# Window-attention backward: from 16x8 token tiles with on-array transposes to stacked 8x8 pairs with DMA transposes

## Chip, core and metric

One NeuronCore of one Trainium2 chip runs the whole program. The metric is the device time of one execution in microseconds (us), the median over runs. Below, PE is the matrix engine (with PEld its weight loads), DVE the vector engine, ACT the scalar engine, POOL and SP the two engines that here mostly issue DMAs.

## What is computed

The image has 256x256 tokens with 384 channels. It is cut into 8x8 windows; within each window there is softmax attention over its 64 tokens, forward and backward:

```python
xw  = windows(x)                                   # [1024 windows, 64 tokens, 384]
q, k, v = split(xw @ wqkv)                         # wqkv [384, 1152]
p   = softmax(q @ k.T * 384**-0.5)                 # 64x64 per window
out = unwindow((p @ v) @ wo)                       # wo [384, 384]
_, vjp = jax.vjp(f, x, wqkv, wo)
return out, *vjp(grad_out)                         # out, dx, dwqkv, dwo
```

All arrays are bfloat16; four results are written.

## The kernel before

Both kernels first fold the weights: A = scale*Wq*Wk^T and its transpose give scores from x alone, and B = Wv*Wo and its transpose give the output and the gradient, so no q, k or v is ever formed. The weight gradients are accumulated as x^T U and x^T W in float32 (`G_acc`, `F_acc`) and turned into dwqkv and dwo after the loop.

Before, a tile is 128 tokens: 8 rows by 16 columns of the image, that is two windows side by side whose tokens are interleaved (8 of one, 8 of the other). The 128x128 score matrix therefore has both windows' scores in a checkerboard, and a fourth matmul (`maskU`, `maskV`, L221) adds a large negative number where the windows cross. The loops run over 32 bands of 8 rows (`band_body`), 4 quads of 4 tiles in each band (128 quads of 512 tokens in all), and in each quad the stages `stage_f1`, `stage_f2`, `stage_b1`, `stage_b2`, `stage_b3` over its 4 tiles. For each quad:

- L173 and L175 load x and grad_out (SP and POOL issue), L180 and L182 transpose them on PE, L183 copies them out of PSUM.
- L190 and L196 project the quad by A and B (rows of 512 columns); L210 transposes the second result back.
- L216 scores, L224 exponential, L244 transposes P, L248 forms the output, L259 to L273 the score gradient, L277 and L282 the operands U and W of the weight gradient, L300 and L305 three transposed products, and L316 the nine matmuls of dx.
- After every 16 tiles, L331 runs 6 chains of 16 matmuls (`ps_dw`) for the weight gradients.

Tile pools give the buffers, and a scheduler of the framework sets the order of instructions on each engine, interleaving neighbouring quads. The quads are written out in full: the program has no loop at run time.

Of the kernel before, what the change touches and what calls it, by code (L numbers as in the profile page):

```python
# [8 lines left out]
ACT = mybir.ActivationFunctionType  # L9
ALU = mybir.AluOpType  # L10
AX = mybir.AxisListType
# [5 lines left out]
def kernel(  # L17
# [10 lines left out]
    dynamic_loop: bool = True,  # L28
    TPB: int = 4,
    NBI: int = 32, HINT_ENGINES=(),  # L30
    GRPN: int = 16, MASK_MM: bool = True, YT_ACT: bool = False, WT_ACT: bool = False, SMALL_ACT: bool = False, XB_ACT: bool = False,
):
    nc = tc.nc
    B, H, W, C = x.shape
    assert B == 1
    P = 128
    CK = C // P
    assert CK * P == C
    WIN = 8
    NB = H // WIN  # L40
    TW = 16
    NTB = W // TW
    assert NTB * TW == W and NB * WIN == H
    QUAD = min(4, NTB)
    GRP = min(GRPN, NTB)
    assert NTB % GRP == 0 and GRP % QUAD == 0
    NGB = NTB // GRP
    QPG = GRP // QUAD
    scale = float(C) ** -0.5
    J = 3 * C  # L50
    JK = J // P
    NBI = min(NBI, NB)
    while NB % NBI != 0:
        NBI -= 1

    const = ctx.enter_context(tc.tile_pool(name="const", bufs=1))
    setup = ctx.enter_context(tc.tile_pool(name="setup", bufs=1))
    qpool = ctx.enter_context(tc.tile_pool(name="qpool", bufs=2))
    gpool = ctx.enter_context(tc.tile_pool(name="gpool", bufs=2))
    tp = ctx.enter_context(tc.tile_pool(name="tp", bufs=TPB))  # L60
    sp = ctx.enter_context(tc.tile_pool(name="sp", bufs=2 * TPB))
    psq = ctx.enter_context(tc.tile_pool(name="psq", bufs=2, space=bass.MemoryType.PSUM))
    psf1 = ctx.enter_context(tc.tile_pool(name="psf1", bufs=1, space=bass.MemoryType.PSUM))
    psf2 = ctx.enter_context(tc.tile_pool(name="psf2", bufs=1, space=bass.MemoryType.PSUM))
    psb1 = ctx.enter_context(tc.tile_pool(name="psb1", bufs=1, space=bass.MemoryType.PSUM))
    psb2 = ctx.enter_context(tc.tile_pool(name="psb2", bufs=1, space=bass.MemoryType.PSUM))
    psb3 = ctx.enter_context(tc.tile_pool(name="psb3", bufs=1, space=bass.MemoryType.PSUM))
    psdw = ctx.enter_context(tc.tile_pool(name="psdw", bufs=1, space=bass.MemoryType.PSUM))

    ident = const.tile([P, P], BF16)  # L70
    make_identity(nc, ident[:])

    w_sb = const.tile([P, CK, J], BF16)
    nc.sync.dma_start(out=w_sb[:], in_=wqkv.rearrange("(m p) j -> p m j", p=P))
    wo_sb = setup.tile([P, CK, C], BF16)
    nc.scalar.dma_start(out=wo_sb[:], in_=wo.rearrange("(m p) n -> p m n", p=P))

    wqkvT_sb = setup.tile([P, JK, C], BF16, tag='setup_big')
    for jm in range(JK):
        ps_t = psq.tile([P, C], BF16, tag="q")  # L80
        for m in range(CK):
            nc.tensor.transpose(ps_t[:, m * P:(m + 1) * P], w_sb[:, m, jm * P:(jm + 1) * P], ident[:])
        nc.vector.tensor_copy(out=wqkvT_sb[:, jm, :], in_=ps_t[:])
    woT_sb = const.tile([P, CK, C], BF16)
    for mco in range(CK):
        ps_t = psq.tile([P, C], BF16, tag="q")
        for mc in range(CK):
            nc.tensor.transpose(ps_t[:, mc * P:(mc + 1) * P], wo_sb[:, mc, mco * P:(mco + 1) * P], ident[:])
        nc.vector.tensor_copy(out=woT_sb[:, mco, :], in_=ps_t[:])

    Bm_sb = const.tile([P, CK, C], BF16)
    for mcin in range(CK):
        ps_c = psq.tile([P, C], F32, tag="q")
        for mc in range(CK):
            nc.tensor.matmul(ps_c[:], lhsT=wqkvT_sb[:, 2 * CK + mc, mcin * P:(mcin + 1) * P], rhs=wo_sb[:, mc, :],
                             start=(mc == 0), stop=(mc == CK - 1))
        nc.vector.tensor_copy(out=Bm_sb[:, mcin, :], in_=ps_c[:])
    A1_sb = const.tile([P, CK, C], BF16)
    for mcin in range(CK):
        ps_c = psq.tile([P, C], F32, tag="q")  # L100
        for mc in range(CK):
            nc.tensor.matmul(ps_c[:], lhsT=wqkvT_sb[:, CK + mc, mcin * P:(mcin + 1) * P], rhs=wqkvT_sb[:, mc, :],
                             start=(mc == 0), stop=(mc == CK - 1))
        nc.scalar.activation(out=A1_sb[:, mcin, :], in_=ps_c[:], func=ACT.Copy, scale=scale)
    A2_sb = const.tile([P, CK, C], BF16)
    for mcin in range(CK):
        ps_c = psq.tile([P, C], F32, tag="q")
        for mc in range(CK):
            nc.tensor.matmul(ps_c[:], lhsT=wqkvT_sb[:, mc, mcin * P:(mcin + 1) * P], rhs=wqkvT_sb[:, CK + mc, :],
                             start=(mc == 0), stop=(mc == CK - 1))  # L110
        nc.scalar.activation(out=A2_sb[:, mcin, :], in_=ps_c[:], func=ACT.Copy, scale=scale)
    A3_sb = const.tile([P, CK, C], BF16)
    for mco in range(CK):
        ps_c = psq.tile([P, C], F32, tag="q")
        for mc in range(CK):
            nc.tensor.matmul(ps_c[:], lhsT=wo_sb[:, mc, mco * P:(mco + 1) * P], rhs=wqkvT_sb[:, 2 * CK + mc, :],
                             start=(mc == 0), stop=(mc == CK - 1))
        nc.vector.tensor_copy(out=A3_sb[:, mco, :], in_=ps_c[:])

    u_f = const.tile([1, P], F32)  # L120
    nc.gpsimd.iota(u_f[:], pattern=[[0, 8], [1, 2], [0, 8]], base=0, channel_multiplier=0,
                   allow_small_or_imprecise_dtypes=True)
    u_b = const.tile([1, P], BF16)
    nc.vector.tensor_scalar(out=u_b[:], in0=u_f[:], scalar1=-2.0, scalar2=1.0, op0=ALU.mult, op1=ALU.add)
    ps_m = psq.tile([P, P], F32, tag="q")
    nc.tensor.matmul(ps_m[:], lhsT=u_b[:], rhs=u_b[:], start=True, stop=True)
    u2_f = const.tile([P, P], F32)
    nc.gpsimd.iota(u2_f[:], pattern=[[0, 8], [1, 2], [0, 8]], base=0, channel_multiplier=4,
                   allow_small_or_imprecise_dtypes=True)
    maskU = const.tile([P, P], BF16)  # L130
    maskV = const.tile([P, P], BF16)
    tmpm = const.tile([P, P], F32)
    nc.vector.tensor_scalar(out=tmpm[:], in0=u2_f[:], scalar1=-2.0, scalar2=1.0, op0=ALU.mult, op1=ALU.add)
    nc.gpsimd.affine_select(out=tmpm[:], in_=tmpm[:], pattern=[[0, P]], compare_op=ALU.is_ge, fill=0.0,
                            base=0, channel_multiplier=-1)
    nc.vector.tensor_copy(out=maskU[:], in_=tmpm[:])
    nc.vector.tensor_scalar(out=maskV[:], in0=tmpm[:], scalar1=2048.0, scalar2=None, op0=ALU.mult)
    nmask = const.tile([P, P], F32)
    nc.vector.tensor_scalar(out=nmask[:], in0=ps_m[:], scalar1=-15000.0, scalar2=15000.0, op0=ALU.mult, op1=ALU.add)

    G_acc = const.tile([P, CK, C], F32)
    F_acc = const.tile([P, CK, C], F32)
    nc.vector.memset(G_acc[:], 0.0)
    nc.gpsimd.memset(F_acc[:], 0.0)

    def dram_tile(ap, b, bt):
        if isinstance(b, int):
            rows = slice(WIN * b, WIN * b + WIN)
        else:
            rows = bass.ds(b * WIN, WIN)  # L150
        return ap[0, rows, TW * bt:TW * bt + TW, :]

    def iter_body(it):
        for sbi in range(NBI):
            b = it * NBI + sbi
            band_body(b)

    def band_body(b):
        for grp in range(NGB):
            x_toks = []  # L160
            do_toks = []
            U_sbs = []
            W_sbs = []
            for q in range(QPG):
                bt0 = grp * GRP + q * QUAD
                xdT_quad = qpool.tile([P, 2, CK, QUAD * P], BF16)
                xT_quad = xdT_quad[:, 0, :, :]
                doT_quad = xdT_quad[:, 1, :, :]
                for bi in range(QUAD):
                    bt = bt0 + bi  # L170
                    gi = bt - grp * GRP
                    x_tok = gpool.tile([P, C], BF16, tag=f"x_tok{gi}")
                    nc.sync.dma_start(out=x_tok[:], in_=dram_tile(x, b, bt))  # L173
                    do_tok = gpool.tile([P, C], BF16, tag=f"do_tok{gi}")
                    nc.gpsimd.dma_start(out=do_tok[:], in_=dram_tile(grad_out, b, bt))  # L175
                    x_toks.append(x_tok)
                    do_toks.append(do_tok)
# [243 lines left out]
```

## Time and profile before

| what | value |
|---|---|
| median of 3 runs | 3115.81 us (3114.57 to 3115.82) |
| profiled execution, first to last instruction (span) | 3115.0 us |
| PE busy, PE weight loads | 3041.1 us (98%), 1867.8 us (60%) |
| DVE, ACT, POOL busy | 2020.5 (65%), 1527.4 (49%), 614.2 us (20%) |
| matmuls, all instructions | 23935, 64454 |
| DMA | 208.43 MB, mean 67 GB/s |

The profile is of one execution; its own time is known as its span, which lies inside the three runs' range. Busy time of PE counts each matmul from its start to a modelled end, and successive matmuls overlap, so 98% does not say that the array is full: the distance between the starts of neighbouring matmuls says more. A line number such as L316 is the line of the kernel that issued the instruction.

### The profile page before, as it was taken

How to read it: one execution, taken by the hardware profiler on the slowest of the kernel's cores; microseconds unless marked ns; L12 is line 12 of the kernel's file. 1: busy time of each engine (PE TensorE's matmuls, PEld its weight loads, DVE VectorE, ACT ScalarE, POOL GpSimd, SP SyncE). 2: the span in 40 equal slices, each digit the busy share in tenths (PEclk: the TensorE clock that was granted, in tenths of full speed). 3: DMA queues.
4: the chain of work that ended last, by engine and by line, in shares of the span. 5: the costliest groups of instructions: out<-in, count | busy, mean ns of one | idle time of the engine just before them, and what ended most of it. 6: DMA issues, size and time to landing. Idle time of an engine off the chain costs nothing.

```text
span 3115.0 us, 64454 instructions
## 1 busy us (share of the span) xinstructions
PE 3041.1 (98%) x23935; PEld 1867.8 (60%) x23935; DVE 2020.5 (65%) x6758; ACT 1527.4 (49%) x3981; POOL 614.2 (20%) x1034
## 2 busy tenths in 40 slices
PE   8999999999999999999999999999999999999998
PEld 5565656666666656666566656566665656656564
DVE  6666766667666666666666666766666666667665
ACT  4445544445444454444554444544445444455443
POOL 4122111122111121111211212211112111121100
PEclk9999999999999999999999999999999999999999
DMA  4222222212222122222222221222212222222211
GB/s 129 68 63 64 71 69 69 70 52 76 68 70 69 52 76 69 70 68 60 65 71 70 71 66 54 76 68 70 70 53 74 68 70 69 62 65 71 58 33 40
DMA packets 206716, 208.43 MB, mean 67 GB/s; under 512 B 49216, under 2 KB 181056, under 8 KB 206400
## 3 DMA queue, kind: packets, MB, share of 16 engines
q0 software_dynamic: 65536, 101.25, 12.2%
q1 hardware_dynamic: 140464, 102.76, 11.2%
q8 instruction: 187, 3.06, 0.4%
q14 instruction: 129, 1.06, 0.1%
q10 hardware_dynamic: 400, 0.29, 0.0%
HBM read 101.84 MB, written 101.84 MB: 65 GB/s over the span
## 4 chain that ended last, share of the span: by engine, by line
PE 88%; DVE 4%; issue 4%; ACT 3%; DMA 0%; ACTq 0%
PE ps_dx L316 24%; PE ps_dw L331 13%; PE ps_p L190 8%; PE ps_p L196 8%; PE ps_t L300 5%; PE ps_W L282 4%; PE ps_w L305 4%; PE ps_xB L210 3%; PE ps_dP L259 3%; PE ps_U L277 3%; PE ps_S L216 3%; PE ps_out L248 2%; DVE xdT_quad L183 2%; PE ps_xdT L180 2%; PE ps_xdT L182 2%
## 5 line engine op out<-in xcount | busy, mean ns | idle before, releaser
L316 PE MATMUL ps_dx<-A_sb,uvwT_sb 128*128 128x384 bf16 x3072 | 703.6, 326 | 0.1
L175 POOL DMA_DIRECT2D do_tok<-in_grad_out_dram x512 | 300.6, 588 | 1429.1 <-PE ps_w L305 1247.3
L302 ACT CAST uvwT_sb<-ps_t 128x512 bf16<-128x512 f32 (+1 forms) x1024 | 498.9, 487 | 85.8 <-PE ps_t L300 82.4
L321 POOL DMA_DIRECT2D out_dram<-dx_sb x512 | 311.2, 608 | 1040.5 <-ACT dx_sb L320 1008.0
L284 DVE CAST W_sb<-ps_W 128x384 bf16<-128x384 f32 x512 | 284.2, 555 | 300.2 <-PE ps_W L282 295.4
L320 ACT CAST dx_sb<-ps_dx 128x384 bf16<-128x384 f32 x512 | 248.7, 486 | 391.1 <-PE ps_dx L316 327.4
L331 PEld LDWEIGHTS <-x_tok 128*128 128x128 bf16 x3072 | 296.5, 97 | 220.5 <-issue 49.2
L250 ACT CAST out_sb<-ps_out 128x384 bf16<-128x384 f32 x512 | 246.7, 482 | 357.1 <-PE ps_out L248 196.8
L316 PE MATMUL ps_dx<-A_sb,wT_sb 128*128 128x384 bf16 x1536 | 378.7, 328 | 0.0
L279 ACT CAST U_sb<-ps_U 128x384 bf16<-128x384 f32 x512 | 246.0, 481 | 268.5 <-PE ps_U L277 266.8
L196 PE MATMUL ps_p<-xdT_quad,Bm_sb 128*128 128x512 bf16 x1152 | 370.4, 379 | 0.1
L190 PE MATMUL ps_p<-xdT_quad,A_sb 128*128 128x512 bf16 x1152 | 364.3, 378 | 4.4 <-DVE xdT_quad L183 4.2
L224 ACT ACTIVATE pe<-ps_S,nmx 128x128 f32<-128x128 f32 x512 | 190.9, 373 | 320.4 <-DVE nmx L223 319.7
L300 PE MATMUL ps_t<-dSS_sb,x_tok 128*128 128x256 bf16 x1536 | 334.2, 272 | 1.0
L331 PE MATMUL ps_dw<-U_sb,x_tok 128*128 128x384 bf16 x1536 | 327.4, 325 | 0.6 <-DVE G_acc L333 0.6
L316 PEld LDWEIGHTS <-uvwT_sb 128*128 128x128 bf16 x3072 | 273.0, 97 | 90.8 <-issue 8.8
L307 DVE CAST wT_sb<-ps_w 128x384 bf16<-128x384 f32 x512 | 283.1, 553 | 46.8 <-PE ps_w L305 44.8
L192 DVE CAST yT_sb<-ps_p 128x512 bf16<-128x512 f32 x384 | 263.8, 687 | 58.2 <-PE ps_p L190 45.2
L198 ACT CAST xBT_sb<-ps_p 128x512 bf16<-128x512 f32 x384 | 229.5, 598 | 120.6 <-PE ps_p L196 117.3
L183 DVE COPY xdT_quad<-ps_xdT 128x768 bf16<-128x768 bf16 x512 | 278.8, 549 | 6.9 <-PE ps_xdT L182 2.6
L331 PE MATMUL ps_dw<-W_sb,x_tok 128*128 128x384 bf16 x1536 | 265.0, 325 | 1.4 <-DVE F_acc L333 0.8
L212 DVE COPY xB_sb<-ps_xB 128x384 bf16<-128x384 bf16 x512 | 181.4, 354 | 115.5 <-PE ps_xB L210 109.0
(93 smaller groups left out, 4732.5 us busy)
## 6 DMA issues: line engine op xcount, KB each, us to landing
x_tok<-in_x_dram SPq DMA_DIRECT2D x512, 96.0 KB
do_tok<-in_grad_out_dram POOLq DMA_DIRECT2D x512, 96.0 KB, 2.7
out_dram<-out_sb SPq DMA_DIRECT2D x512, 96.0 KB
out_dram<-dx_sb POOLq DMA_DIRECT2D x512, 96.0 KB, 2.5
w_sb<-in_wqkv_dram SPq DMA_DIRECT2D x1, 864.0 KB
out_dram<-dwqkv_sb SPq DMA_DIRECT2D x1, 864.0 KB
wo_sb<-in_wo_dram ACTq DMA_DIRECT2D x1, 288.0 KB
out_dram<-ep_t SPq DMA_DIRECT2D x1, 288.0 KB
```

The source lines that it names most:

```text
L175: nc.gpsimd.dma_start(out=do_tok[:], in_=dram_tile(grad_out, b, bt))
L183: nc.vector.tensor_copy(out=xdT_quad[:, :, :, bi * P:(bi + 1) * P], in_=ps_xdT[:].rearrange("p a (m t) -> p a m t", m=CK))
L190: nc.tensor.matmul(ps_p[:], lhsT=A2_sb[:, m, mq * P:(mq + 1) * P], rhs=xT_quad[:, m, :], start=(m == 0), stop=(m == CK - 1))
L192: (nc.scalar.copy if YT_ACT else nc.vector.tensor_copy)(out=yT_sb[:, mq, :], in_=ps_p[:])
L196: nc.tensor.matmul(ps_p[:], lhsT=Bm_sb[:, m, mco * P:(mco + 1) * P], rhs=xT_quad[:, m, :], start=(m == 0), stop=(m == CK - 1))
L284: nc.vector.tensor_copy(out=W_sb[:], in_=ps_W[:])
L300: nc.tensor.matmul(ps_t[:, i, :], lhsT=x_tok[:, mc * P:(mc + 1) * P], rhs=dSS_sb[:].rearrange("p a t -> p (a t)"), start=True, stop=True)
L302: nc.scalar.copy(out=uvwT_sb[:, mc0:mc0 + nm, :], in_=ps_t[:, 0:nm, :])
L307: (nc.scalar.copy if WT_ACT else nc.vector.tensor_copy)(out=wT_sb[:], in_=ps_w[:])
L316: nc.tensor.matmul(ps_dx[:], lhsT=srcT[:, mc, o0:o0 + P], rhs=A_sb[:, mc, :], start=(k == 0), stop=(k == 3 * CK - 1))
L321: nc.gpsimd.dma_start(out=dram_tile(out_1, b, bt), in_=dx_sb[:])
L331: nc.tensor.matmul(ps_dw[:], lhsT=x_toks[ti][:, ma * P:(ma + 1) * P], rhs=srcs[ti][:], start=(ti == 0), stop=(ti == GRP - 1))
```

## The change

The kernel is rewritten. A tile is now 16 rows by 8 columns: two windows stacked, one in partitions 0 to 63, the other in 64 to 127, so the windows never mix and no mask is needed. A quad is 4 such tiles (16x32 tokens), and there are again 128 quads. What differs in the work:

- x and grad_out (`turn_in`) and the two projections (`turn_yh`) are transposed by DMA, four transposing DMAs of 128x1536 elements a quad, issued by SP. The projections are x by A and grad_out by B^T.
- Scores, the score gradient and everything of P runs in pieces of the array: scores as 128x64 (the whole contraction, half the columns), `md`, `attn` and `turn_p` as 64x64 pieces, each with its own weight load.
- Tiles of one quad share one softmax on 128x256 elements (`chain1` to `chain3`); PSUM is emptied by 10 copies of 512 or 768 columns a quad on DVE and 11 on ACT, instead of smaller ones for each tile.
- `attn` forms U and W. The output and one of the three terms of dx come from `MD` (x transposed, times P and the score gradient) by B or A^T; `attn` adds the other two terms in the same PSUM banks.
- The weight gradient is taken over 3 quads (12 matmuls a chain), two of six chains in each step.
- All buffers are fixed rings, PSUM banks are named by hand, and the order on every engine is that of `step(n)`: it works on quad n (`T`), the scores of n+1 (`S`), the projection of n+2 (`A`), the transposes of n+3 and the loads of n+4.

The new part, cut to what the prediction speaks of (all matmuls are issued by the helper `mm`, L73, and all copies by `ev`, L77 on ACT and L79 on DVE; the tests by which `step` leaves stages out in its first and last steps are cut):

```diff
+    NX, ND, NXT, NDT, NYH, NTOK, NVW = 11, 5, 3, 2, 2, 3, 6
+    def load(n):
+        for t in range(4):
+            SP.dma_start(out=X[:, (n % NX) * 4 + t, :], in_=img(x, n, t))
+            SP.dma_start(out=DO[:, (n % ND) * 4 + t, :], in_=img(grad_out, n, t))
+    def turn_in(n):
...
+        SP.dma_start_transpose(out=XT[:, n % NXT, :, :], in_=xs)
...
+        SP.dma_start_transpose(out=DOT[:, n % NDT, :, :], in_=ds)
+    def turn_yh(n, a):
+        SP.dma_start_transpose(out=YH[:, n % NTOK, a, :, :],
+                               in_=YHT[:, n % NYH, a, :, :].rearrange("p m t -> p (m t)"))
+    def proj(n, a, banks, engs):
...
+        for mo in range(CK):
+            o = PS[:, banks[mo], :]
+            for m in range(CK):
+                mm(o.rearrange("p (t k) -> p t k", t=4), wgt[:, m, mo * P:(mo + 1) * P], src[:, m, :, :],
+                   m == 0, m == CK - 1)
+            ev(engs[mo], YHT[:, n % NYH, a, mo, :], o)
+    def scores(n):
+        for a in range(2):
+            for t in range(4):
+                for m in range(CK):
+                    for w in range(2):
+                        r = slice(64 * w, 64 * w + 64)
+                        mm(PS[r, 6, a * 256 + t * 64:a * 256 + t * 64 + 64],
+                           YHT[:, n % NYH, a, m, t * P + w * 64:t * P + w * 64 + 64],
+                           XT[:, n % NXT, t * CK + m, r], m == 0, m == CK - 1)
...
+    def md(n):
+        for m in range(CK):
+            for t in range(4):
+                for hh in range(2):
+                    for w in range(2):
+                        r = slice(64 * w, 64 * w + 64)
+                        mm(PS[64 * hh:64 * hh + 64, 2 * m + w, t * P:t * P + P],
+                           X[r, (n % NX) * 4 + t, m * P + hh * 64:m * P + hh * 64 + 64],
+                           TT[r, n % 2, t, :, :], True, True)
...
+    def attn(n, t, bvw, bdx):
...
+            for cr in range(2):
+                for w in range(2):
+                    r = slice(64 * w, 64 * w + 64)
+                    o = 64 * (w if cr == 0 else 1 - w)
+                    if cr == 0:
+                        mm(PS[o:o + 64, bvw + a, 0:C], PB[r, n % 2, a, t, :], src[r, :], True, True)
+                    else:
+                        mm(PS[o:o + 64, bdx, 0:C].rearrange("p (m k) -> p m k", m=CK), PB[r, n % 2, a, t, :],
+                           yh[r], a == 0, False)
...
+        def step(n):
+            T, S, A = n, n + 1, n + 2
...
+                load(n + 4)
+                turn_in(n + 3)
+                scores(S)
+                chain1(S)
+                md(T)
+                wgrad(g, k0)
+                chain2(S)
+                chain3(S)
+                outs(T, 0, 0, ACT)
+                outs(T, 2, 2, DVE)
+                outs_st(T)
+                proj(A, 0, (4, 5, 0), (ACT, DVE, ACT))
+                turn_yh(A, 0)
+                wgrad(g, k0 + 1)
+                attn(T, 0, 2, 4)
+                attn_ev(T, 0, 2, DVE)
+                attn(T, 1, 0, 5)
+                attn_ev(T, 1, 0, ACT)
+                dxs(T, 0, 4, ACT)
+                dxs_st(T, 0)
+                proj(A, 1, (2, 3, 1), (DVE, ACT, DVE))
+                turn_yh(A, 1)
+                turn_p(S)
+                turn_p_ev(S)
+                attn(T, 2, 2, 4)
+                attn_ev(T, 2, 2, ACT)
+                attn(T, 3, 0, 5)
+                attn_ev(T, 3, 0, DVE)
+                dxs(T, 2, 4, ACT)
+                dxs_st(T, 2)
+        for n in range(-3, GQ * NG + GQ):
+            step(n)
```

The arguments after `t` in `attn` and the tuples in `proj` are PSUM banks and the engines that empty them. `outs` and `dxs` are 12 matmuls of 384 columns each a quad, `wgrad(g, k)` is one chain of 12. `outs_st` issues 4 and `dxs_st` 8 stores a quad on POOL (L177, L207); a wait named DMAHW0 to DMAHW7 or DMASW0 to DMASW7 is for one of 8 semaphores that the DMAs of a kind use in turn, so that a DMA also waits for the eighth one before it.

Where the change moves instructions: the order of PE in the middle of the program before, where one quad's scores, output, U and the transposed product stand beside each other:

```order
L216 LDWEIGHTS yT_sb
L216 MATMUL ps_S<-xdT_quad,yT_sb 128x128
L221 LDWEIGHTS maskU
L221 MATMUL ps_S<-maskV,maskU 128x128
L248 LDWEIGHTS PT_sb
L248 MATMUL ps_out<-xB_sb,PT_sb 128x384
L277 LDWEIGHTS dSS_sb
L277 MATMUL ps_U<-x_tok,dSS_sb 128x384
```

The order of PE now, from the end of a weight-gradient chain into `attn`, with its waits (PB holds P and the score gradient, YH the transposed projections):

```order
L73 MATMUL PS<-VW,X 128x384
L73 LDWEIGHTS PB
L73 MATMUL PS<-X,PB 64x384 [waits DVE_49]
L73 LDWEIGHTS PB
L73 MATMUL PS<-X,PB 64x384
L73 LDWEIGHTS PB [waits DMAHW6_49]
L73 MATMUL PS<-YH,PB 64x384 [waits Activation_49]
```

What was one matmul over the whole array (L277) is now several over quarters of it, and PE waits here for a transposing DMA as well as for DVE and ACT.

The order of DVE in a step now (ST, SS, TM, PEX are the softmax's small tiles, OS the output, TT the transposed P):

```order
L79 CAST VW<-PS 128x768
L128 TENSOR_REDUCE ST<-PS 128x4
L129 TENSOR_TENSOR SS<-PS,ST 128x256
L79 CAST MD<-PS 128x4x128 x3
L219 TENSOR_TENSOR ACC<-PS,ACC 128x384
L136 TENSOR_REDUCE ST<-PEX 128x4
L137 RECIPROCAL ST<-ST 128x4
L138 TENSOR_TENSOR PB<-PEX,ST 128x256
L139 TENSOR_TENSOR TM<-PS,PB 128x256
L140 TENSOR_REDUCE ST<-TM 128x4
L79 CAST OS<-PS 128x768
L79 CAST YHT<-PS 128x512
```

The softmax of the next quad now stands between the copies that free PSUM for the present one.

SP's queue before, in the middle of the program:

```order
L173 DMA x_tok<-in_x_dram 128x1x384 x9
L251 DMA out_dram<-out_sb 8x16x384
L173 DMA x_tok<-in_x_dram 128x1x384 x5
L251 DMA out_dram<-out_sb 8x16x384
L173 DMA x_tok<-in_x_dram 128x1x384 x2
```

SP's queue now, the second half of one step's loads and its four transposes, with their waits:

```order
L91 DMA X<-in_x_dram 128x1x384 [waits DMAHW0_49]
L92 DMA DO<-in_grad_out_dram 128x1x384 [waits DMAHW1_49,PE_49]
L91 DMA X<-in_x_dram 128x1x384 [waits DMAHW2_49]
L92 DMA DO<-in_grad_out_dram 128x1x384 [waits DMAHW3_49,PE_49]
L96 DMA_TRANSPOSE XT<-X 128x12x128 [waits DMAHW4_49]
L98 DMA_TRANSPOSE DOT<-DO 128x12x128 [waits DMAHW5_49]
L101 DMA_TRANSPOSE YH<-YHT 128x12x128 [waits DMAHW6_49,DVE_49,Activation_49]
L101 DMA_TRANSPOSE YH<-YHT 128x12x128 [waits DMAHW7_49,DVE_49,Activation_49]
```

The stores have gone from SP to POOL, grad_out's loads from POOL to SP, and every load now stands behind transposes that wait for DVE and ACT.

More of the change, by code (lines that the diff above doesn't have):

```diff
@@ L4 @@
 import concourse.tile as tile
[L5 removed]
+from concourse import mybir
 from concourse._compat import with_exitstack
 from concourse.masks import make_identity
[L9 removed]
+ACTF = mybir.ActivationFunctionType
 ALU = mybir.AluOpType
@@ L66 @@
[L66 to L75, printed above, removed]
@@ L91 @@
[L91 to L104, printed above, removed]
@@ L105 @@
[L105 to L118, printed above, removed]
@@ L138 @@
[L138 to L151, printed above, removed]
@@ L353 @@
-    Gb = eptile('yT_sb')
-    nc.vector.tensor_copy(out=Gb[:], in_=G_acc[:])
-    Fb = eptile('yT_sb')
-    nc.vector.tensor_copy(out=Fb[:], in_=F_acc[:])
-    GTb = eptile('xBT_sb')
-    FTb = eptile('xBT_sb')
-    for src, dst in ((Gb, GTb), (Fb, FTb)):
-        for mb in range(CK):
-            ps_t = psq.tile([P, C], BF16, tag="q")
-            for ma in range(CK):
-                nc.tensor.transpose(ps_t[:, ma * P:(ma + 1) * P], src[:, ma, mb * P:(mb + 1) * P], ident[:])
-            nc.vector.tensor_copy(out=dst[:, mb, :], in_=ps_t[:])
@@ L382 @@
[L382 to L390 removed]
+    NQC = W // 32
@@ new lines @@
+    NQ = (H // 16) * NQC
+    scale = float(C) ** -0.5
+    GQ = 3
+    NG = (NQ + GQ - 1) // GQ
+    NX, ND, NXT, NDT, NYH, NTOK, NVW = 11, 5, 3, 2, 2, 3, 6
+    PE, DVE, ACT, POOL, SP = nc.tensor, nc.vector, nc.scalar, nc.gpsimd, nc.sync
+    sb = ctx.enter_context(tc.tile_pool(name="sb", bufs=1))
+    pp = ctx.enter_context(tc.tile_pool(name="pp", bufs=1, space=bass.MemoryType.PSUM))
+    PS = pp.tile([P, 8, 512], F32, name="PS")
+    X = sb.tile([P, NX * 4, C], BF16, name="X")
+    DO = sb.tile([P, ND * 4, C], BF16, name="DO")
@@ new lines, in wgrad @@
+    def wgrad(g, k):
+        quads = range(g * GQ, min(NQ, (g + 1) * GQ))
+        which, ma = k // CK, k % CK
+        tiles = [(q, t) for q in quads for t in range(4)]
+        for i, (q, t) in enumerate(tiles):
+            mm(PS[:, 7, 0:C], X[:, (q % NX) * 4 + t, ma * P:(ma + 1) * P], VW[:, (q % NVW) * 4 + t, which, :],
+               i == 0, i == len(tiles) - 1)
+        if g == 0:
+            DVE.tensor_copy(out=ACC[:, k, :], in_=PS[:, 7, 0:C])
+        else:
+            DVE.tensor_tensor(out=ACC[:, k, :], in0=PS[:, 7, 0:C], in1=ACC[:, k, :], op=ALU.add)
```

439 lines of the change are left out of this document (163 added, 276 removed).

## The prediction

> **What bounds the kernel now.** I read the page first: the shares of the engines, then the chain that ended last and the granted clock, then the steady stretch alone.
>
> ```profile
> span 3115.0 us, 64454 instructions
> PE 3041.1 (98%) x23935; PEld 1867.8 (60%) x23935; DVE 2020.5 (65%) x6758; ACT 1527.4 (49%) x3981; POOL 614.2 (20%) x1034
> ...
> PEclk9999999999999999999999999999999999999999
> ...
> PE 88%; DVE 4%; issue 4%; ACT 3%; DMA 0%; ACTq 0%
> ```
>
> PE is busy 98%, carries 88% of the chain, and has its full clock. Next come the windows of the loop and the rows at its ends.
>
> ```profile
> 21.90 0.33 PE L180 MATMUL ps_xdT<-ident,x_tok 128*128 128x128 bf16 x3 [0.35 <-DVE A_sb L118]
> ...
> 22.00:3102.00 3080.00, 3018.92 (x23828) 1855.76 (x23828) 2007.11 (x6729) 1520.27 (x3968) 597.74 (x1001) 1.00 0.24 66
> ...
> 3101.80 0.65 PE L369 MATMUL ps_e<-w_sb,ep_t 128*128 128x384 bf16 x3
> ```
>
> The loop runs from 21.9 to 3101.8: 24.06 us for each of 128 quads; the last 13.2 us are the end. In the window's row the columns after PE and PEld are DVE, ACT and POOL; then the clock 1.00, the DMA share 0.24 and 66 GB/s. What PE needs is read from the timeline, where several like matmuls stand in one row.
>
> ```profile
> 1511.31 0.33 PE L216 MATMUL ps_S<-xdT_quad,yT_sb 128*128 128x128 bf16 x3
> ...
> 1502.94 0.38 PE L300 MATMUL ps_t<-dSS_sb,x_tok 128*128 128x256 bf16 x2
> ...
> 3093.13 2.76 PE L331 MATMUL ps_dw<-W_sb,x_tok 128*128 128x384 bf16 x16 [0.31 <-DVE F_acc L333]
> ...
> 1515.28 1.24 PE L190 MATMUL ps_p<-xdT_quad,A_sb 128*128 128x512 bf16 x5
> ```
>
> ```profile
> L331 PE MATMUL ps_dw<-W_sb,x_tok 128*128 128x384 bf16 x1536 | 265.0, 325 | 1.4 <-DVE F_acc L333 0.8 <-DVE G_acc L333 0.6
> ...
> L300 PE MATMUL ps_t<-dSS_sb,x_tok 128*128 128x256 bf16 x1536 | 334.2, 272 | 1.0
> ...
> L190 PE MATMUL ps_p<-xdT_quad,A_sb 128*128 128x512 bf16 x1152 | 364.3, 378 | 4.4 <-DVE xdT_quad L183 4.2
> ...
> L216 PE MATMUL ps_S<-xdT_quad,yT_sb 128*128 128x128 bf16 x1536 | 173.6, 218 | 10.2 <-DVE xB_sb L212 6.2
> ```
>
> A row's length less one matmul's mean, divided by one less than the count, is the distance of starts, with a weight load in each: (0.33-0.218)/2 = 0.056 us for 128 columns, (0.38-0.272)/1 = 0.108 for 256, (2.76-0.325)/15 = 0.162 for 384, (1.24-0.378)/4 = 0.216 for 512. A quad has, by the code, 84, 12, 72 and 18 of these: 4.70 + 1.30 + 11.66 + 3.89 = 21.55 us. So of 24.06 us the array's stream takes 21.55 and waits hidden inside the modelled ends 2.5.
>
> **The change, PE.** Kept at full width are 48 matmuls of 384 (24 weight-gradient, 12 `outs`, 12 `dxs`) and 18 of 512: 7.78 + 3.89 = 11.67 us. All 84 of 128 and 12 of 256 columns go (transposes, mask, scores, L259, L300, L305), and so do U, W and most of dx at full width. In their place come pieces, which no row shows:
>
> - 112 small pairs of load and matmul: 48 scores (64 columns), 48 `md` (128 columns, quarter array), 16 transposes. Upper end: each like the 128-column pair, 0.056. Lower end: half the columns, 0.028. No row shows two PE instructions in less than 0.056, so I take that, the nearest row: 6.27 us (lower 3.14).
> - 32 matmuls of 384 in `attn`, four on the four quarters of the array in turn. Upper end: one after another, 32 x 0.162 = 5.18. Lower end: four at once, 1.30. If they overlap, instructions still come at 0.056 a pair: 1.79, which I take since it uses the fastest rate a row shows and still assumes overlap, the unproved step.
>
> Sum 11.67 + 6.27 + 1.79 = 19.73 us a step, with ends 16.1 and 23.1.
>
> **What must keep up.** The copies:
>
> ```profile
> L284 DVE CAST W_sb<-ps_W 128x384 bf16<-128x384 f32 x512 | 284.2, 555 | 300.2 <-PE ps_W L282 295.4
> L192 DVE CAST yT_sb<-ps_p 128x512 bf16<-128x512 f32 x384 | 263.8, 687 | 58.2 <-PE ps_p L190 45.2
> L250 ACT CAST out_sb<-ps_out 128x384 bf16<-128x384 f32 x512 | 246.7, 482 | 357.1 <-PE ps_out L248 196.8
> L198 ACT CAST xBT_sb<-ps_p 128x512 bf16<-128x512 f32 x384 | 229.5, 598 | 120.6 <-PE ps_p L196 117.3
> L224 ACT ACTIVATE pe<-ps_S,nmx 128x128 f32<-128x128 f32 x512 | 190.9, 373 | 320.4 <-DVE nmx L223 319.7
> L223 DVE TENSOR_REDUCE nmx<-ps_S 128x1 f32<-128x128 f32 x512 | 145.8, 285 | 35.9 <-PE ps_S L221 29.7
> L321 POOL DMA_DIRECT2D out_dram<-dx_sb x512 | 311.2, 608 | 1040.5 <-ACT dx_sb L320 1008.0
> ```
>
> 128 columns more cost DVE 0.132 and ACT 0.116 us, so 768 take 0.95 and 0.83. DVE in a step: 6 copies of 512 (4.12), 3 of 768 (2.85), transposed P (below 0.69), two accumulations (like 384, 1.11), and the softmax, six operations on 256 columns at 0.285 + 0.132 and a reciprocal (below 0.3): 2.8. Sum 11.6. ACT: 6 of 512 (3.59), 5 of 768 (4.15), the exponential (0.49): 8.2. POOL: 12 stores at 0.608 = 7.3, plus two operations on 256 columns without a row. All stay below 19.7.
>
> The waits in a step, at these durations: scores end at 2.7 us, `md` at 5.4, the first weight-gradient chain at 7.3. DVE reduces and subtracts till 3.5, copies MD till 6.1 while `outs` needs it at 7.3 (slack 1.2). DVE then adds till 7.9, ends the softmax at 9.8, copies OS till 10.8; `attn` overwrites that bank at 13.2 (slack 2.4). The tightest is `proj(A, 1)` at 15.0, for which DVE must have copied the first VW after the second accumulation: 13.2 + 0.56 + 0.95 = 14.7. POOL's two operations have from 9.8 to 17.0, so up to 3.6 us each costs nothing. So nothing must wait, but margins of 0.3 us are thin. Bounds for waits are 0 and the 2.5 of before; I take a quarter, 0.6.
>
> A step changes 7 times between pieces and full width or one kind of piece and another (scores to `md`, to full width, to `attn`, back, to `turn_p`, `attn` to `dxs`, to scores). No row shows such a change. Bounds: nothing, as between any two matmuls of before; or PE empties first, which loses the part of a matmul that overlaps the next, 0.218 - 0.056 = 0.162 us, 1.13 a step. I take nothing and keep the other end as a rival. The Trainium skill speaks for that rival: by TensorEngine Tiling, section Tiling Modes (Key Properties), changing the tiling mode drains TensorE; the sum below would be 2795 by the rule and is 2650 without it.
>
> **The change, DMA and SP.** The plain traffic stays: 0.24 x 24.06 = 5.8 us of all DMA engines a quad. New are four transposing DMAs of 384 KB, 1.57 MB, as much as the plain traffic; at the same rate 5.8 us more, together 0.57 of a 20.3 us step. SP issues 8 loads and 4 transposes a step.
>
> ```profile
> 0.81 0.45 SPq L74 DMA_DIRECT2D w_sb<-in_wqkv_dram  x1
> ...
> do_tok<-in_grad_out_dram POOLq DMA_DIRECT2D x512, 96.0 KB, 2.7
> ```
>
> A load costs SP 0.45 us, 3.6 a step. A transposing issue has no row: at least one issue, 0.45; at most one for each of its 12 blocks of 128x128, 5.4. I take the first, nearest as one instruction of the same kind; SP is then at 5.4 us a step. The order hides its landing (2.7 us for a plain load): XT and YH are used a step or more after they are issued. With 8 semaphores for 12 DMAs, the last loads of a step wait for the transposes of the step before, and SP's queue behind them too; that costs nothing while SP has slack. DO's slot frees at the end of the step before, also in time. By the Trainium skill, DMA: Bandwidth & Descriptors, section Latency and other measured facts, DMA transposes move 261 GB/s; an estimate from it is 1.5 us for each, and the sum would be unchanged; no run here shows it yet.
>
> **The sum.** A step 19.73 + 0.6 = 20.33 us; 128 steps 2602. Ends: the setup as before 22; three filling steps, whose own matmuls are 3.9 and 7.5 us (projections; then scores and transposes too) and which wait for three landings in turn (8), 20; steps 0 to 2 lack 3 x 3.9 of weight gradient (-11.7), 126 and 127 lack projections and one set of scores (-11.4); four steps follow with weight gradients alone (15.6), and the end 13.2. Together 48, nearly all PE. 2602 + 48 = 2650 us, against the span of 3115.0 that this execution had, 0.8 below the median of the runs. Within 0.2%, 6 us, would be called no change.
>
> **Rivals.**
> 1. PE empties at each change of piece: 128 x 1.13 = 145 more, 2795. Nothing in the trace speaks for or against; no matmul before is on part of the array. Chance 0.2.
> 2. The pieces don't overlap: `attn` 5.18 instead of 1.79, step 23.7, 3085 us, still faster by a little; with the drains or the waits of before it passes 3115. For it: each matmul before starts only when the last one's columns are in. Against: quarters share no rows and no PSUM partitions of a bank. Chance 0.1, half of it slower.
> 3. The other side: transposes bound SP. At the upper end, 12 x 0.45 each, SP needs 4 x 5.4 + 3.6 = 25.2 us a step: 3226 + 48 = 3274, slower. It decides from (3115-48)/128 = 23.96 a step, that is 5.1 us for one transposing DMA; above 4.2 it already sets the step. DMA engines would do the same if transposes ran at 0.3 of the plain rate. For it: SP is in order, and transposes that wait for DVE and ACT hold all loads behind them. Against: both queues are at 0.24 share now. Chance 0.14, of which 0.11 slower.
>
> What remains, 0.56, is the forecast (2180 to 2890 by the ends of the pairs and waits). The range reaches from 2180, a step near the lower ends of the pairs, to 3050, which takes in the drains, part of the serial pieces and a mild SP bound. Faster 0.83, same 0.01, slower 0.16.
>
> **What would show it.** Right: starts of 128-column `md` matmuls 0.056 us apart or less, four `attn` matmuls in about 0.22, steps of 20.3 us, DVE near 11.6 and ACT near 8.2 us a step, DMA share near 0.57, clock full. Wrong: PE waiting for XT or YH by DMA, SP's queue without gaps, `attn` starts 0.162 apart, or a granted clock below 1 because PE idles. That can happen: in the end of before PE stood for 1.0 of 2.5 us, and in the next stretch its clock (the first number after the pairs) was 0.50.
>
> ```profile
> 3100.00:3102.50 2.50, 1.48 (x14) 0.99 (x15) 1.66 (x4) 0.02 (x1) 0.00 (x0) 0.99 0.04 7
> 3102.50:3105.60 3.10, 3.10 (x11) 1.51 (x10) 0.56 (x1) 1.27 (x3) 0.00 (x0) 0.50 0.00 0
> ```

## The result: 2075.98 us, a third faster, and below the stated range

| | median | runs |
|---|---|---|
| before, same chip | 3115.41 us | 3114.57 to 3115.82 |
| changed kernel | 2075.98 us | 2074.48 to 2076.58 |
| ratio | 0.6663 | 95% interval 0.6654 to 0.6673 |

The head of the changed kernel's page, its chain, and the steady window; the window's columns are those explained before.

```profile
span 2072.7 us, 65934 instructions
PE 2029.9 (98%) x26970; PEld 1149.4 (55%) x26970; DVE 1358.6 (66%) x2452; ACT 985.1 (48%) x1555; POOL 1012.9 (49%) x1798
...
PEclk9999999999999999999999999999999999999999
...
PE 96%; DMA 2%; SPq 2%; DVE 0%; ACT 0%; issue 0%; DVEq 0%
```

```profile
500.00:1500.00 1000.00, 999.65 (x13341) 567.76 (x13340) 672.65 (x1214) 486.39 (x767) 505.33 (x895) 1.00 1.06 203
```

PE is the bound again: 96% of the chain, full clock. Most of one step in PE's timeline (start, length, count):

```profile
1015.20 0.95 PE L73 MATMUL PS<-XT,YHT 128*64 128x64 bf16 x48
1016.08 0.86 PE L73 MATMUL PS<-TT,X 64*64 64x128 bf16 x48
1016.87 2.12 PE L73 MATMUL PS<-VW,X 128*128 128x384 bf16 x12
...
1024.77 0.35 PE L73 MATMUL PS<-X,PB 64*64 64x384 bf16 x2
1024.77 0.35 PE L73 MATMUL PS<-YH,PB 64*64 64x384 bf16 x2
1024.95 0.33 PE L73 MATMUL PS<-DO,PB 64*64 64x384 bf16 x2
...
1025.28 0.33 PE L73 MATMUL PS<-DO,PB 64*64 64x384 bf16 x2
...
1026.53 2.11 PE L73 MATMUL PS<-DOT,BT_sb 128*128 128x512 bf16 x9
1028.57 0.38 PE L150 MATMUL PS<-ident,PB 64*64 64x64 bf16 x12
...
1030.85 0.95 PE L73 MATMUL PS<-XT,YHT 128*64 128x64 bf16 x48
```

A step is 1030.85 - 1015.20 = 15.65 us; over 116 steps, from a `scores` row at 90.52 to one at 1907.71, it is 15.66. 128 x 15.66 = 2004.5, and 68 us of the span are ends. The pieces' means come from the groups by shape:

```profile
L73 PE MATMUL PS<-XT,YHT 128*64 128x64 bf16 x6144 | 121.6, 197 | 1.0 <-DVE TT L79 0.7 <-DVE YHT L79 0.2
L73 PE MATMUL PS<-TT,X 64*64 64x128 bf16 x6144 | 110.8, 218 | 0.3 <-ACT DXS L77 0.3
```

By the prediction's own formula the starts lie (0.95 - 0.197)/47 = 0.016 us apart in `scores`, (0.86 - 0.218)/47 = 0.0137 in `md`, and (0.38 - 0.195)/11 = 0.017 in `turn_p` (0.195 is its mean), a weight load with each. 0.0137 is a quarter of the 0.056 that 128 columns took over the whole array. In `attn` four matmuls, two X and two YH on the four quarters, start together at 1024.77; from the DO at 1024.95 to the DO at 1025.28 two such fours go by, 0.165 us each.

The four transposes are dear for SP. Its queue over most of the same step (a row can hold waits too, and one of x2 also the time between the two):

```profile
1012.28 2.47 SPq L96 DMA_TRANSPOSE XT<-X  x1
1014.80 2.58 SPq L98 DMA_TRANSPOSE DOT<-DO  x1
1017.49 5.24 SPq L101 DMA_TRANSPOSE YH<-YHT  x2
1022.78 0.58 SPq L91 DMA_DIRECT2D X<-in_x_dram  x1
...
1027.98 1.77 SPq L96 DMA_TRANSPOSE XT<-X  x1
```

From the first XT to the next are 15.7 us without a gap: 10.3 for four transposes, the rest for eight loads at about 0.65. Over the whole run the medians of single transposes are 2.11 us for XT, 2.60 for DOT and 2.42 for YH, so this step is a little above them.

### The profile page after: what moved, and what is told of

Read it like the earlier page. It is cut to its first block, busy times and chain, and to the rows that moved or that the text cites. A ratio compares the mean times of both kernels' runs of the same rounds, so it can differ in the third digit from the quotient of the medians.

```text
span 2072.7 us, 65934 instructions
## 1 busy us (share of the span) xinstructions
PE 2029.9 (98%) x26970; PEld 1149.4 (55%) x26970; DVE 1358.6 (66%) x2452; ACT 985.1 (48%) x1555; POOL 1012.9 (49%) x1798
## 4 chain that ended last, share of the span: by engine, by line
PE 96%; DMA 2%; SPq 2%; DVE 0%; ACT 0%; issue 0%; DVEq 0%
PE PS L73 94%; PE PS L150 2%; DMA XT<-X 1%; SPq L92 0%; SPq L91 0%; SPq L231 0%; DMA VW<-in_wo_dram 0%; DVE ACC L219 0%; SPq L233 0%; ACT DXS L77 0%; ACT YHT L77 0%; SPq L98 0%; DVE YHT L79 0%; SPq L96 0%; PE PS L310 0%
## 5 line engine op out<-in xcount | busy, mean ns | idle before, releaser
L207 POOL DMA_DIRECT2D out_dram<-DXS x1024 | 572.8, 566 | 583.7 <-ACT DXS L77 561.4
L73 PE MATMUL PS<-VW,X 128*128 128x384 bf16 x3072 | 542.7, 326 | 4.5 <-DVE ACC L219 4.5
L73 PEld LDWEIGHTS <-X 64*64 64x64 bf16 (+1 forms) x9216 | 380.3, 104 | 218.8 <-issue 6.9
L79 DVE CAST YHT<-PS 128x512 bf16<-128x512 f32 x384 | 264.3, 688 | 240.4 <-PE PS L73 238.4
L73 PEld LDWEIGHTS <-MD 128*128 128x128 bf16 x3072 | 279.3, 98 | 232.4 <-issue 61.5
L77 ACT CAST VW<-PS 128x768 bf16<-128x768 f32 x256 | 204.3, 798 | 367.6 <-PE PS L73 367.6
L77 ACT CAST YHT<-PS 128x512 bf16<-128x512 f32 x384 | 224.7, 585 | 277.6 <-PE PS L73 253.7
L73 PE MATMUL PS<-AT_sb,MD 128*128 128x384 bf16 x1536 | 294.1, 328 | 0.0
L73 PE MATMUL PS<-XT,A_sb 128*128 128x512 bf16 x1152 | 273.7, 383 | 10.4 <-DMA XT<-X 10.2
L177 POOL DMA_DIRECT2D out_dram<-OS x512 | 276.1, 545 | 13.9 <-issue 11.4
L73 PE MATMUL PS<-B_sb,MD 128*128 128x384 bf16 x1536 | 271.5, 326 | 4.3 <-DVE MD L79 2.5
L73 PE MATMUL PS<-DOT,BT_sb 128*128 128x512 bf16 x1152 | 270.5, 380 | 0.0
L77 ACT CAST DXS<-PS 128x768 bf16<-128x768 f32 x256 | 204.3, 798 | 138.3 <-PE PS L73 138.3
L79 DVE CAST VW<-PS 128x768 bf16<-128x768 f32 x256 | 244.0, 953 | 18.6 <-PE PS L73 4.8
L79 DVE CAST MD<-PS 128x512 bf16<-128x512 f32 x384 | 240.2, 681 | 0.6 <-PE PS L73 0.6
L73 PE MATMUL PS<-YH,PB 64*64 64x384 bf16 x2048 | 238.6, 332 | 1.0 <-ACT DXS L77 1.0
L77 ACT CAST MD<-PS 128x512 bf16<-128x512 f32 x384 | 200.1, 594 | 67.1 <-DVE ST L128 64.6
L77 ACT CAST OS<-PS 128x768 bf16<-128x768 f32 x128 | 102.1, 798 | 194.5 <-PE PS L73 194.5
L73 PEld LDWEIGHTS <-A_sb 128*128 128x128 bf16 x1152 | 113.4, 99 | 135.6 <-issue 12.4
L73 PEld LDWEIGHTS <-BT_sb 128*128 128x128 bf16 x1152 | 113.1, 98 | 123.8 <-issue 2.4
```

Of the source, the lines that this page charges most:

```text
L73: PE.matmul(out, lhsT=lhsT, rhs=rhs, start=start, stop=stop, skip_group_check=True)
L77: ACT.copy(out=out, in_=in_)
L79: DVE.tensor_copy(out=out, in_=in_)
L177: POOL.dma_start(out=img(out_0, n, t), in_=OS[:, n % 2, t, :])
L207: POOL.dma_start(out=img(out_1, n, t)[8 * w:8 * w + 8], in_=DXS[64 * (1 - w):64 * (1 - w) + 64, n % 2, t, :])
```

## The experiments

The first question was what lets the pieces overlap, and whether their order matters; the second what a change of piece costs; the third who else is near the bound. Each edit is to the changed kernel unless said otherwise. All but `ends` and `ends_dopool` (five runs each) are single runs; the changed kernel's own four lie within 2.1 us.

**Order of the pieces.** Three runs put matmuls of the same part of the array behind each other.

```diff
 # attn_q: in attn            # md_q: in md                  # sc_q: in scores
-for a in range(2):           -for t in range(4):            -for m in range(CK):
-    for cr in range(2):      -    for hh in range(2):       -    for w in range(2):
-        for w in range(2):   -        for w in range(2):    +for w in range(2):
+for cr in range(2):          +for hh in range(2):           +    for m in range(CK):
+    for w in range(2):       +    for w in range(2):
+        for a in range(2):   +        for t in range(4):
```

> In attn the two matmuls of one quarter of the array now follow each other (quarter outermost, operand innermost); nothing else changes, the results are the same. If quarters overlap and matmuls start in program order, eight matmuls of a tile take 5 x 0.162 = 0.81 us instead of 2 x 0.162 = 0.33, 0.49 us more for each of 512 tiles: 2076 + 248 = 2324 us. If small matmuls are merely issued faster, wherever they lie, nothing changes: 2076.

> In md the four matmuls of a run (128 columns) now use the same quarter, and the quarter changes only between runs. Overlap by place: a run takes 3 x 0.056 + 0.014 = 0.18 us, 12 runs 2.2 us a step instead of 0.66, so 128 x 1.5 = 195 us more, 2270, if nothing else hides it. Merely faster issue: 2076.

> In scores the three matmuls of a sum (64 columns, half the array) now follow each other on one half. Overlap by place: 2 x 0.029 + 0.016 = 0.074 us for three instead of 0.048, 16 x 0.026 = 0.42 us a step, 2076 + 53 = 2130 us. If each of them cost 0.056 as the prediction took for pieces that do not overlap, 16 x (2 x 0.056 + 0.016) = 2.05 instead of 0.77: 2240. Merely faster issue: 2076.

Measured: 2097.61, 2089.23 and 2075.59 us; none came near its price for serial pieces. The timeline of attn_q says why:

```profile
1020.66 0.35 PE L73 MATMUL PS<-X,PB 64*64 64x384 bf16 x2
1020.68 0.35 PE L73 MATMUL PS<-YH,PB 64*64 64x384 bf16 x2
1020.85 0.33 PE L73 MATMUL PS<-DO,PB 64*64 64x384 bf16 x2
1020.86 0.33 PE L73 MATMUL PS<-YH,PB 64*64 64x384 bf16 x2
...
1025.07 0.32 PE L73 MATMUL PS<-X,PB 64*64 64x384 bf16 x1
1025.39 0.32 PE L73 MATMUL PS<-DO,PB 64*64 64x384 bf16 x1
1025.39 0.35 PE L73 MATMUL PS<-X,PB 64*64 64x384 bf16 x1
```

Its code issues X, DO, X, DO and then four with YH. PE started both X and two YH within 0.04 us and DO 0.17 later: pieces whose part of the array was free went ahead of an earlier one whose part was busy. So these orders could not take the overlap away: the 48 matmuls of `md` take 0.94 us in md_q instead of 0.86, and those of `scores` 0.96 in sc_q instead of 0.95. The 22 us that attn_q lost are 0.18 in each step (15.84 us), and the last three rows, for the fourth tile, show where: DO waits for a PSUM bank that DVE still copies (the wait that `ends` below removes), and the second X, behind it in the program but by the code on another quarter, starts only with it. So a piece passed one that waited for its part of the array, but not one that waited for another engine. The step of md_q is 15.73 us, 0.07 more, about what its `md` row lost; the rest of its 13 us was not followed.

**One quarter for all.** All pieces of `md` and `attn` use the first quarter, so that nothing can overlap. Half their products are left out and others made twice; count and columns are the same.

```diff
-                        r = slice(64 * w, 64 * w + 64)
-                        mm(PS[64 * hh:64 * hh + 64, 2 * m + w, t * P:t * P + P],
+                        r = slice(0, 64)
+                        mm(PS[0:64, 2 * m + w, t * P:t * P + P],
...
-                    o = 64 * (w if cr == 0 else 1 - w)
+                    o = 0
```

> All pieces of md and attn are put on one quarter of the array (both windows read the first 64 partitions and write the first 64), so half of the products are left out and the others computed twice; the count and shape of the instructions stay. If a piece takes its quarter for its columns and the gain is that four quarters work at once: md 48 x 0.056 = 2.69 us instead of 0.66, attn 32 x 0.162 = 5.2 instead of 1.3, 5.9 us more a step, 2076 + 760 = 2836 us. If small pieces are cheap wherever they are: 2076. The run with the quarter outermost changed little, because PE started matmuls of other quarters ahead; here there is no other quarter.

Measured: 2790.57, 715 us or 5.6 a step more; 5.9 were expected. Its timeline:

```profile
1010.94 0.49 PE L73 MATMUL PS<-X,PB 64*64 64x384 bf16 x2
1011.26 0.49 PE L73 MATMUL PS<-YH,PB 64*64 64x384 bf16 x2
1011.59 0.48 PE L73 MATMUL PS<-DO,PB 64*64 64x384 bf16 x2
...
1015.59 2.87 PE L73 MATMUL PS<-TT,X 64*64 64x128 bf16 x48
```

`md` starts are now (2.87 - 0.216)/47 = 0.0565 apart (0.216 is its mean here), and two `attn` matmuls take 0.325 us, 0.163 each. These are the before kernel's distances for 128 and 384 columns: in `md` and `attn` a piece costs what its columns cost, and the gain is that four quarters run at once. `scores` and `turn_p` still overlap in this run, so for their pieces of 64 columns no run shows the serial price.

**Changes of piece.** The first weight-gradient chain of a step is cut in three and put between the parts of `md`: the same work, four more changes a step.

```diff
 def md(n, g=None, k=0):
     for m in range(CK):
...
+        if g is not None:
+            wgrad_part(g, k, 4 * m, 4 * m + 4)
```

> The first weight-gradient chain of a step is cut in three pieces of four matmuls that stand between the three parts of md: the same matmuls, four more changes between quarter pieces and full width in a step (11 instead of 7). If a change costs the 0.11 us that the gaps in the trace suggest: 128 x 0.44 = 56 us, 2132. If it costs a whole emptying, 0.162: 2159. If it costs nothing: 2076, or a little less, since DVE gets more time between its copies.

Measured: 2135.75, so 60 us, 0.47 a step, 0.117 for each change (a step in the middle of the loop went from 15.66 to 16.15 us, 0.12 for each).

```profile
1012.78 0.42 PE L73 MATMUL PS<-TT,X 64*64 64x128 bf16 x16
1013.13 0.82 PE L73 MATMUL PS<-VW,X 128*128 128x384 bf16 x4
1013.88 0.42 PE L73 MATMUL PS<-TT,X 64*64 64x128 bf16 x16
```

The period is 13.88 - 12.78 = 1.10; 16 x 0.0137 and 4 x 0.162 make 0.87, and the rest is 2 x 0.117. The Trainium skill, TensorEngine Tiling (Array Packing), section Tiling Modes (Key Properties), says that changing the tiling mode drains TensorE; the run agrees that a change costs time, 0.117 us, and does not show whether PE drains in it.

**Less PE work.** Every other tile is left out of the weight gradients, 1.95 us of PE a step; then also grad_out's transpose (the projection reads x transposed instead); then grad_out's transpose alone, with PE's work whole; then the first edit with grad_out loaded by POOL.

```diff
 # half_w, half_w_nodot, half_w_dopool
-        tiles = [(q, t) for q in quads for t in range(4)]
+        tiles = [(q, t) for q in quads for t in (0, 2)]
 # half_w_nodot, nodot
-        SP.dma_start_transpose(out=DOT[:, n % NDT, :, :], in_=ds)
 # half_w_dopool
-            SP.dma_start(out=DO[:, (n % ND) * 4 + t, :], in_=img(grad_out, n, t))
+            POOL.dma_start(out=DO[:, (n % ND) * 4 + t, :], in_=img(grad_out, n, t))
```

> Leaves out every other tile in the weight gradients (12 matmuls of 384 columns less a step). PE then needs 15.66 - 1.95 = 13.7 us a step. If PE alone bounds the kernel: 2076 - 250 = 1826 us. If the DMA engines, whose packets sum to 1.06 of the time, or SP are at their limit too: 2000 to 2076. In between (1830 to 2000) means that DMA or SP sets the step as soon as PE is a little faster.

> As half_w, and grad_out is not transposed either: the second projection reads x transposed in its place, one transposing DMA of four less. If half_w stayed above 1826 because of DMA or SP, this falls to about 1826. If PE alone counts, both are equal.

> The changed kernel without the transposes of grad_out (the second projection reads x transposed in its place); PE's work is whole. If PE's own stream is 15.6 us a step and bounds as closely as the DMAs do: 2060 to 2076 us. If the transposes alone set the step: 15.66 - 2.45 = 13.2, at least below 1950.

> As half_w (every other tile left out of the weight gradients), and grad_out is loaded by POOL instead of SP: the same bytes, four issues of 0.6 us a step less on SP. If SP's issuing set the step of half_w: about 1900 us, where its copies on DVE hold PE (the run without grad_out's transposes was 1919). If the DMA engines are full: 2080 again.

Measured: half_w 2083.11, half_w_nodot 1919.15, nodot 2066.01, half_w_dopool 1918.31. PE's longest wait of the loop in half_w, then in half_w_dopool:

```profile
PE PS L73 <- DMA XT<-X: 133.4, 86, 4.4
```

```profile
PE PS L73 <- DVE MD L79: 63.7, 250, 0.9
```

With less work for PE, half_w gains nothing: its steps vary from 14.53 to 21.39 us while PE waits for XT. With four loads taken off SP and the same bytes moved, the step falls to an even 14.53 us, held then by DVE's copies of MD. So SP's queue and not the DMA engines was in the way, though their share in the steady window reads 1.15 there. The loads' issue time and their waits for PE left SP together, and the run does not part the two. With PE's work whole, nodot's step is 15.66 like the changed kernel's; its 10 us come from the ends.

**One more transpose**, a fifth transposing DMA a step, into a buffer nobody reads; and the same with grad_out's loads on POOL.

```diff
                 turn_yh(A, 0)
+                SP.dma_start_transpose(out=JT[:], in_=YHT[:, A % NYH, 0, :, :].rearrange("p m t -> p (m t)"))
```

> One more transposing DMA a step, into a buffer that nobody reads. By the trace a transpose takes about 2.7 us of all 16 DMA engines (84.1% of the span on that queue, less the plain loads' 16%, over 512) and 2.5 us of SP. If the DMA engines are full: 15.66 + 2.7 = 18.4 us a step, 2420 us. If SP is full: about 2400. If both have slack of that size: 2076. If they have half of it: 2200 to 2300.

> The run with one more transposing DMA a step, and now grad_out is loaded by POOL instead of SP. If the 2.44 us that the extra transpose cost is SP's time to issue it, four loads of about 0.6 us (2.4 us) leave SP's queue and its step returns to about 15.6 us: about 2080 us. If the DMA engines are the limit (their share was 1.02 in that run), the bytes are the same and the time stays near 2390.

Measured: 2388.4 and 2203.57. The first is 2.44 us a step more. In the second neither number came out: four loads fewer gave back 1.44. SP's queue in the second, without a gap again:

```profile
1015.18 2.09 SPq L102 DMA_TRANSPOSE YH<-YHT  x1
1017.32 3.46 SPq L276 DMA_TRANSPOSE JT<-YHT  x1
1020.88 2.01 SPq L102 DMA_TRANSPOSE YH<-YHT  x1
1022.95 2.94 SPq L92 DMA_DIRECT2D X<-in_x_dram  x4
1025.99 1.58 SPq L97 DMA_TRANSPOSE XT<-X  x1
```

A transpose's time on SP depends on where it stands: over this run the median is 1.95 us for XT, which follows four loads, and 3.24 for JT, right behind another transpose. So the extra one is not a fixed price, and how much of it is the DMA engines stays open.

**Before with DMA transposes alone.** In the kernel before, x and grad_out are transposed by eight DMAs of 128x384 a quad instead of by L180 to L183.

```diff
-                    ps_xdT = psq.tile([P, 2, C], BF16, tag="q")
-                    for m in range(CK):
-                        nc.tensor.transpose(ps_xdT[:, 0, m * P:(m + 1) * P], x_tok[:, m * P:(m + 1) * P], ident[:])
...
+                    nc.sync.dma_start_transpose(out=xdT_quad[:, 0, :, bi * P:(bi + 1) * P], in_=x_tok[:])
+                    nc.sync.dma_start_transpose(out=xdT_quad[:, 1, :, bi * P:(bi + 1) * P], in_=do_tok[:])
```

> The kernel before with one part of the change alone: x and grad_out are transposed by DMA (eight transposing DMAs of 128x384 a quad, from SP) instead of by 24 matmuls and 4 DVE copies. PE loses 24 x 0.056 = 1.34 us of 24.06 a quad: 3115 - 172 = 2943 us if the waits stay as they are. If the DMA transposes are the reason for the gain, much less than that, 2400 or below. If SP's order makes the loads late: 3115 or above.

Measured: 3651.44, 536 us slower than before. The chain's shares, and two of its waits (us in total, times, longest):

```profile
PE 58%; SPq 19%; DMA 11%; issue 9%; ACT 1%; POOL 1%; DVE 1%; POOLq 0%; ACTq 0%
```

```profile
PE ps_p L185 <- DMA xdT_quad<-x_tok: 253.4, 67, 7.3
SPq L246 <- ACT out_sb L245: 407.0, 158, 9.2
```

SP takes its queue in order: a store that waits for ACT (L246) holds the transposes behind it, and PE waits for those. It is what the prediction's third rival feared, DMAs stuck behind one that waits, in the old order of the queue. The changed kernel issues its transposes a step or more ahead and has no store on SP; that this is why it escapes is argued from the two orders and not tested. What the DMA transposes are worth in the new order, against transposes on PE, no run shows.

**A shorter start and one copy moved** (`ends`): loads of the first quads go to ACT's queue too, the filling steps transpose before they load, and the last copy of `proj(A, 1)` goes from DVE to ACT. Then grad_out's loads of the loop go to POOL as well (`ends_dopool`).

```diff
-            SP.dma_start(out=X[:, (n % NX) * 4 + t, :], in_=img(x, n, t))
-            SP.dma_start(out=DO[:, (n % ND) * 4 + t, :], in_=img(grad_out, n, t))
+            (ACT if n == 1 else SP).dma_start(out=X[:, (n % NX) * 4 + t, :], in_=img(x, n, t))
+            (ACT if n < 2 else SP).dma_start(out=DO[:, (n % ND) * 4 + t, :], in_=img(grad_out, n, t))   # ends_dopool: else POOL
...
-                proj(A, 1, (2, 3, 1), (DVE, ACT, DVE))
+                proj(A, 1, (2, 3, 1), (DVE, ACT, ACT))
```

> A version meant to be faster: the second projection's last copy goes to ACT instead of DVE (attn of the fourth tile waits about 0.1 us for it in each step), the first two quads are loaded with help of ACT's queue, and in the filling steps the transposes are issued ahead of the next loads. Against the changed kernel's 2076: about 8 us for the start, and 128 x 0.1 = 13 more if PE sets the step: 2055. If the DMAs set it, only the start: 2068.

> The kernel with the shorter start, and grad_out's loads of the loop on POOL. If PE alone sets the step now, SP's relief changes nothing: 2055 to 2062 us, as the shorter start alone. If SP still delays single steps, about 10 us less, near 2050. If POOL's stores come late behind its loads, more than 2065.

Measured: ends 2059.66 us, ratio to before 0.6609 (0.6600 to 0.6618); ends_dopool 2041.31, ratio 0.6551 (0.6542 to 0.6560). Both beat the changed kernel, by 0.8% and 1.7%. Where the copy mattered shows in `attn` for tiles 2 and 3, in the changed kernel and then in ends_dopool:

```profile
1029.17 0.33 PE L73 MATMUL PS<-X,PB 64*64 64x384 bf16 x2
1029.49 0.35 PE L73 MATMUL PS<-DO,PB 64*64 64x384 bf16 x2
```

```profile
1008.52 0.33 PE L73 MATMUL PS<-X,PB 64*64 64x384 bf16 x2
1008.67 0.35 PE L73 MATMUL PS<-YH,PB 64*64 64x384 bf16 x2
1008.68 0.33 PE L73 MATMUL PS<-DO,PB 64*64 64x384 bf16 x2
```

The gap of 0.32 us from X to DO shrinks to 0.16. It was a wait for PSUM bank 1, which DVE was copying, as its timeline in the changed kernel shows (0.69 us, till 1029.43):

```profile
1028.74 0.69 DVE L79 CAST YHT<-PS 128x512 bf16<-128x512 f32 x1 [0.67 <-PE PS L73]
```

Without it the step is 15.48 us, in most steps of ends and in 113 of the 117 steps of ends_dopool between 96.46 and 1908.04 (1811.58/117 = 15.48): there PE alone sets the step. With grad_out's loads on SP, 117 steps of ends take 7.3 us more, and its waits list XT 12 times. The edit of the start gained little by itself: the second `scores` row stands at 36.29 us in ends instead of 42.55, but then PE waits 5.4 us for XT, and the fifth row is at 89.97 instead of 90.52. Only with grad_out's loads on POOL is it at 80.98. So of the 18 us between the two runs, where 10 or none were expected, about half is the start.

## Why the prediction was right in direction and wrong in size

The step was forecast at 20.33 us and took 15.66:

| term of the step | forecast | measured | by |
|---|---|---|---|
| full-width matmuls | 11.67 | 11.67 | distances 0.162 and 0.216 in the step's rows |
| 112 small pairs | 6.27 | 1.70 | 48 x 0.016 + 48 x 0.0137 + 16 x 0.017 |
| `attn`, 32 matmuls | 1.79 | 1.30 | 32 x 0.163/4; the fours in the step's rows are 0.165 apart |
| changes of piece | 0 | 0.82 | 7 x 0.117, the price in `inter`; not measured one by one |
| waits | 0.6 | 0.18 | the step of ends and ends_dopool against this one |
| step | 20.33 | 15.67 | |

- **The step that failed is the price of the small pairs**: "each like the 128-column pair, 0.056", with a lower end of 0.028. It missed by 4.6 us a step, 585 us in all. The 0.056 was no limit on how fast PE takes instructions; it was the 128 columns themselves, as one_q shows, where the pieces take 0.0565 on one quarter and 0.0137 on four. That is shown for `md`; for the 64-column pairs of `scores` and `turn_p` it is inferred from their like distances. The prediction had the right argument one bullet further on: for `attn`'s lower end it let four quarters run at once. Applied to the pairs it would have put their lower end at about 0.056/4 x 112 = 1.6 us, near what came out. The range failed with it, since its low end rested on 0.028.
- **`attn` overlaps**, as forecast, and fully. Rival 2 is ruled out: one_q is nearly the kernel that it described (only `scores` and `turn_p` still overlap), and costs 715 us more. Its argument against, that quarters share no rows, was not right: by the code the X and YH matmuls of one window read the same 64 rows, and all four ran at once even so. The Trainium skill, TensorE: Matmul & The Clock Gate, Part 3: Packing small matmuls — row/col tiling, puts a pack of tiles at one matmul's time and about 4 ns for each further tile. Taking the distance of 0.162 for that time, an estimate from it is 0.174 us for four; the fours in the step's rows are 0.165 apart.
- **Rival 1's cost is real**, at 0.117 us instead of its 0.162: 105 us in all, if all seven changes cost alike, which the forecast took at nothing. It was outweighed by the pairs.
- **Waits** came out lower than the quarter that was taken. `proj(A, 1)` was named as the tight place, for its first VW copy; the one wait left is beside it, `attn` waiting for DVE's last copy of that projection.
- **Copies, clock and PE as bound** were right: DVE takes 0.673 x 15.66 = 10.5 us a step (11.6 forecast) and ACT 7.6 (8.2). POOL takes 7.9 and holds nothing.
- **A transposing DMA** was taken at 0.45 us of SP, "nearest as one instruction of the same kind"; it takes 2.1 to 2.6 in the loop (the medians). The prediction's other figure, an estimate of 1.5 us for each, lies below that too. In the step shown SP's rows fill 15.5 us instead of 5.4: its queue had no gaps, a sign that the prediction had named for being wrong, where it relied on slack. The DMA share came out at 1.06, not 0.57. The time didn't show it, since PE needs 15.66; half_w and extra_t do. The third rival would make the kernel slower only above 5.1 us for each DMA, so it was out by a factor of two, not ten.
- **The ends** are 68 us instead of 48. PE's first matmul waits for a weight until 14.0, and five waits for XT take 10.2 us more, 6.1 of it in the first 60 us, while the loads of the first quads go through SP one by one. In ends_dopool they are 2040.4 - 128 x 15.48 = 59.

Where the gain came from: a quad before took 24.06 us on PE, 21.55 of it stream and 2.5 waits. Now the stream is 14.67 with 0.82 for changes and 0.18 for waits. Of the 8.4 us gained, 2.3 are waits; 5.6 hang on the quarters running at once, by one_q, which at 2790.57 us is still faster than before.

## What to carry to other kernels

Price a matmul by its columns, and divide by the number of pieces that run at once: here pieces on the four quarters cost a quarter of the time each, and a change between pieces and full width 0.12 us. When no row shows an operation, take the bound of every piece from the same argument, not from the nearest row for one and from overlap for another. When PE's time falls by a third, look at the queue that issues the DMAs: SP's rows filled 15.5 of 15.66 us and took back all of half_w's 1.95 us, and moving four loads to POOL gave 0.9% (2059.66 to 2041.31 us), about half of it in the start.

## What was not expected of the hardware

- PE starts matmuls out of the program's order when their part of the array is free (attn_q: YH at 1020.68, ahead of a DO that starts at 1020.85). The Trainium skill, TensorE: Matmul & The Clock Gate, Part 3: Packing small matmuls — row/col tiling, says that matmuls start and end in strict order; the rows of attn_q show otherwise for starts.
- A load and a matmul of 128 columns for a quarter of the array every 0.0137 us on average, with four quarters in use (`md`).
- A change between quarter pieces and full width costs 0.117 us (inter).
- A transposing DMA of 128x1536 elements takes SP 2.1 to 2.6 us in the changed kernel (medians; single rows from 1.4 to 4.2), three to four times a plain load at 0.65; and the mean busy share of the DMA engines can read 1.15 while they are not what holds the step (half_w_dopool).
